# One core, top-k attention and mixer MLP: the closing check in five blocks at other places, planner figures for transfers, and a new order of steps

## The chip, the cores and the metric

The kernel runs on one core of a Trainium2 chip. The core has TensorE (PE, with its weight loads shown as PEld), VectorE (DVE), ScalarE (ACT), GpSimd (POOL) and SyncE (SP, which here only issues transfers). Each engine takes its own instructions in program order and waits for others by semaphores. The metric is device time in microseconds (us), from launch to end; smaller is better.

## The reference

Eight batches of eight heads, 576 rows of 64 numbers each. For every row the 32 largest scores are kept, the softmax runs over these, and the result goes through two MLPs, one across the 576 tokens and one across the 512 channels.

```python
scores = scale * np.matmul(q, k.transpose(0, 1, 3, 2))
kth = np.partition(scores, -top_k, axis=-1)[..., -top_k:-top_k + 1]
scores = np.where(scores >= kth, scores, -1000000000.0)
attn = np.exp(scores - np.max(scores, axis=-1, keepdims=True))
attn = attn / (np.sum(attn, axis=-1, keepdims=True) + 1e-09)
x = heads side by side of np.matmul(attn, v)          # 8 x 576 x 512
h = np.maximum(x.transpose(0, 2, 1) @ w_tok1, 0.0) @ w_tok2
u = x + h.transpose(0, 2, 1)
out = u + np.maximum(u @ w_ch1, 0.0) @ w_ch2
```

## The kernel before

**Tiling.** Two heads of a batch make a pair, so there are 32 pairs; a pair has nine tiles of 128 rows by 576 scores, 288 tiles in all, and two tiles are worked on together as a duo. Two pairs share one duo, since 576 is four and a half times 128. `group` takes one or two duos, `front` loads and transposes q and k of a pair, `back` multiplies by v, and `mlp_ops` runs the MLPs of a batch after every fourth pair.

**One duo.** TensorE makes the scores (L553), ScalarE copies them on a grid of whole numbers into the tile SX (L368). VectorE finds the largest values in six segments (L590, L593, L594, L596) and from them a first threshold, with small steps on a handful of numbers (L686, nh). ScalarE counts how many scores lie above it (L608, into `cnt`). GpSimd turns the scores into integers around that threshold (L616, L619), VectorE finds the eight largest of these (L625, into `tlo`), and small steps give the final threshold (L686 nt, L707). Then there are two ways on. Most duos are rescored: GpSimd marks the kept scores in U (L634), TensorE forms the scores once more with the dropped ones pushed down (L563, L569), and ScalarE takes the exponential into Pm (L639). The others (KEEP) have their exponential from before (L601), and GpSimd makes a mask M and multiplies (L645, L649). SP transposes Pm by a transfer into PT (L671). Only the last duo (number 286 of the rows' count) is transposed by TensorE, in `flip` (L662), with a copy by ScalarE (L666) and one by VectorE (L668). `back` multiplies PT by v (L730) into a bank of TensorE's memory, and VectorE divides by the row sums (L744 reciprocal, L747 product, into Xb). The bank is free again after L747.

**The MLPs.** L794 and L809 are the first token product, L829 and L833 the second with the residual, L916 and L949 the first channel product, L868 and L873 the second with the residual; L799, L838, L886, L936, L944 and L962 are ScalarE's copies and ramps behind them, and L881, L889, L954 and L957 VectorE's share in the last batch. The last batch begins part of L916 ahead of time in held chunks.

**The check.** The threshold search holds for data within bounds. At the end the kernel checks the bounds on `cnt`, `thi`, `tlo` and the row sums `rds` and adds the violations in `bad`; TensorE sums them over the 128 rows (L1038), VectorE casts the sum to `flag` (L1041). If the flag is above 0, the whole is computed again by a slow path (L1184 on, not run with these inputs). `judge` (L1007 to L1028) is one step of 21 VectorE instructions, with 6.0 us in the plan; `sums` (L1030) follows after the last division. `tmp` and `ti`, which `judge` writes, lie in the two buffers of sg, the unused output of L608. The inputs of `judge` are complete once the last L625 is done.

**The order.** Each piece of work is a step: `plan.add` gets the engine, a duration, the function that issues the instructions, the steps that it depends on and the buffers that it uses. `ORDER` holds two characters for every step, which give its place. `Plan.run` goes through the steps by place, adds up a time for each engine and each buffer from the durations, picks for every buffer the one that comes free first by this reckoning, and puts warm-up products (`heat`, L1046) into TensorE's gaps. It does not reorder. The dependencies given to `plan.add` enter this reckoning only; the waits in the program are set where instructions touch the same data. `CLOG` is a charge on SP's steps while earlier transfers still run; `dma` of `weight` says how long a transfer of weights occupies the transfer engines in the plan. The weights are issued by GpSimd (`wdma`, L410).

**VectorE's order at the end, before.** The last L625; the last group's L686 and L707; `judge`; L744 and L747 of the pair 30; the copy L668; L744 and L747 of pair 31, in three parts; `sums`; four L954 and four L957; L889; L881; L881; the flag; L881. GpSimd's order at the end: U of duos 282, 280 and the first half of 286; M; a cast of v (L465); M; the second half of U of 286; two L649. TensorE's: L730 of pair 30; the rescores of 280 and 286; L794; L868 in two halves; `flip`; L829; L730 of pair 31 in two parts (40 and 10 products), with held chunks of L916 between; L794; the rest of the MLPs.

Of the kernel before, what the change touches and what calls it, by code (L numbers as in the profile page):

```python
# [19 lines left out]
LOWEST = -(2.0**33) + 2.0**12  # L20
HIGHEST = 2.0**34 - 2.0**12
# [20 lines left out]
    "'$'''c'd'o's(}'l'm(O(r(~$g$o$x%L$}$~%H%0%Y&/&?%$%|%M%/%<&,&:&>&E$h$q%F%G%{%}&)%]&+&0&H%6&%%z&-&'%D&=&M&O&R'5'8':"
    "'9'F'D'L'e'j'h'x(%'k'g'f(-(4(9(C(E(w(y)#(D(F)$)I*&***5*8#3#4#1$/$0$=$>#a&U&W(|'3'2'7'6,?%N%P%W&<&1&w&#&K&~'%'*&5"
    "&8&G&@&I&r'-'0'E%O%Q&C&J&x&o&v&{'&'/'H%_&2&F&N&B&6')'J'O%x'R't'q'r'p('(Z(((,(@(A(=(P(](?(G(B(`(f(h(n)5)G)H)L)Z*("
    ")P)S)Q)V*)%q%t&7&z&D&t&q'#','I'U&P'S&Q'M&}'+'['`'w&j&l&|'V'Q'G'P'W'Z'b'~&n'.'(&p'C&s'K'|($()(J(M(I(L(R(^(i)D)C)E"
    ")b)e)F)R)N)g)m)x*+*-*.*a*c*,*U*b*d*y'?'A'N'a'Y(0(3(1(6(:(<'T']'{'z(#'y(&(*(Q(u(Y({(v)-)<)@)U)O)T)}*;*=*A*H*W*Y*X"
    "*Z*z+J+W+['@'B'^(5(;'_(X(S(a(c),'X'}(+(/(o(p)&)+)4'n'u(8(d(V(U(W(k(m)*)7(7(l(j(g(_(b).)3):)=)X)`)W)[*6*$*4*S*R*Q"
    "*h*m*V+%*T*u+.+4+K+N,$,(,-+O+R,),,,.(H(K(T)8)0)6([)%)?)h)l(e)>);)9)/)f)k)q)s(x(z)))c)n)r)i)1)u)w)|)')2)d)p)o)()t"
    ")z*#*0*[*]*^*_*p*o*v+'+M+&+D+U+(+Q+L+]+`+c,*,+,/,2-#,:,;,O,Q,~-;-G-K(N(q*P*`,%,&-g-j(s(t*g+$,0,3-l.N-m.O.R.U.S.X"
    "/V/Z.n/E/T/^.h/_/U/Y0h1B0i1C0k1@1{1~1|2#2^2m2t333c3{5t5B5|6j5c5f627$$(&X-r)A)B)J)K/?'<*'&S*f*e*~*}-[)M)Y)v)y*M*<"  # L50
    '*3*I*k*n*w)j*1*7*/){*@*B*s+/)])_)~*i*r*C*:*D*t+7+;*9*J*G*E+2*F+6+9+A+#+C+I+H+G+F+_,K+d+l,9,7,8,A,F,<,=,6,L,N,T,p'
    ',q,r,s-(-7-n,z-X,|-Y-s)^)a*2*N*>*?*j*q+=+h+m*K*x*O+5*L*l+:+e+o+)+++0+1+?+3+^+<+f+k+q+8+>+V+Y+X+T+b+p+s+u,4,1,5,R'
    ",a,g,k,v,x,y-0-3,{,},w-=-D-S-]-_.Q.T/8-`-b.Y.f/9+*+,+B+z+j+y+Z+g,G,J,_+@,C+}+w+x,E,I,M,e,',l-9-6-B-M-Q-Z-a-^.A.C"
    '.E.G.I.`.d.c.e/:/a/l/n+-+E+i+v+~+|,D+{,H,`,i+a,B+n+t,#+r,W,f,m,@,P,S,Z,Y,c,V,X,j,n-),U,[,d,^,],b,h,o-?-A-c-d-i-k'
    ".;.3.:.[.].^.o.r._.b.a.z/./2/C/D/b/|00/}/~0/020b-$-'-+---O-.-R-2-U.#.%-*-L-1-,-/-4-V.&.1-:-<-E-I-P-z-|-x.,.5.8-H"
    '-{-}-J-W-T.-.7.<.@.V.k.W.i/(.{/+/</@/=/K/Q/B/>/A/c/e/z0(0)050X0c0,0-0]0^0d1`1e1h*%*|-q,t,u-&-%1E-o-t2a.g.m.j.}4+'
    "-5-8->.*.2.(.0-N.?.t.w-@.)-F.'-~-C.4.6.y-e-f-w.D.9./.K.$.p.s.~-v.=.+.B.M-y.q/#/%.P/)/X/[/F/G/j/g/f/k0&0'0%0:0E0*"
    "0+0$0H0L0P0S0p1I1M1r1t2`1G1J1H1a2_-h-u.>/&.F.H.L.v/-/R/t...u.J/$.x/P/u/w07.l.|/'///*/7/6/4/J/O09/,/1/I/3/0/5/h08"
    "0?0A0[0W0e0Y1.1,141K1N1L1S1[1Q1O1P1j1l1n1x1y2X2]2c1z2Y2d2r3'/;/H/S0@0B/p/i/o0G0R0T/L/N0F/M/d/q0n0q0|/`1+1=1>1R1U"
    "1Z1b1d1c1o2%2,22252Z2e2[2f2n393S3V/W/]/m/s0>/x0C/v0N0U1#/r0V0I0o0O/y0z1*1//{0.0;0Q0l0x0M0=0{1'150<0J0m0u0w0D1$1-"  # L60
    '191<2$1v1A1D2G2B2F2h2i2g2z2}2k2l2j3$3<3@3^3_3z3~443]3`3}4-4503040r121)100t0v181:1]0K131X1%160~1_1m2-060Z0s1&110y'
    '1V0}1q2.211(1W1;1T1^171g1p24292q2p2o2s3#2|3&3-3/3.3B3D3132303F3H3J3a3b4,40464)4*4N4X4l5e6)686f6l6h6n7(7I717Z7X7['
    "7Y7]9#9,9/9490969d9o8~939c9l:D:X9e9n:C:W9g9p:E:Y:~;D;A<(;@;Y;T<*;]<);S;[<'<-<3<4<@<{=@=u@F=5=B=w=A=C=y?8-p*{3(0`"
    "0_0f0g4P0a2b5q3+3*3534700j1?1i2:2)2+2C282L2Q2U1Y1k1f2*2'2E2H2T2W1s1u2&2I2;2(202D2P2S2w2<2V2>2@2=2?2x2{2~363%373Y"
    "3e3Z3j4B3i3p4%4&4$4:4=4'4(4#4?4A4J4L4M4Q4R4s4t5o4S4U4T4V5p1w1}232M272N2K2J2R3C3T2/2v2y2O2A263=3N3m2u3,3?3K3M3I3O"
    '3G3Q3W3r3;3L3>3E3X3A3l3q3t3v484u4/4r595=5@5F5H5G5Q5T5J5K5I5X5[5`5k5l656g6i5j5m6m6~7#383:3P4H3k3U3R3y4[4c4g3h4@3u'
# [102 lines left out]

# [1066 lines left out]
```

## Time and profile before

| | us |
|---|---|
| median of three runs | 744.05 |
| lowest and highest of them | 742.95, 744.85 |
| the profiled execution | 743.19 |
| its span, first to last instruction | 741.2 |

The page gives busy time by engine over the span. A stretch is a part of the span between two times. The order in time lists an engine's instructions as start, duration, engine, line, operation, output and inputs, and in brackets how long the engine was idle before it and what ended that. The chain that ended last is followed back from the last instruction, at each step to what released it. An instruction's busy time holds any stall inside it.

### The profile page before, as it was taken

What the parts mean: (1) busy time and instruction counts of PE and PEld (TensorE: products, weight loads), DVE (VectorE), ACT (ScalarE), POOL (GpSimd) and SP (SyncE); (2) the same over time, 40 slices, a digit from 0 to 9 for tenths busy, and PEclk for the clock granted to TensorE, in tenths of its full rate; (3) what the DMA queues carried; (4) which work ended last, traced back from release to release, by engine and by line L of the source; (5) the groups of instructions that cost most, each with busy time, mean ns of one, the idle gap of its engine ahead of it and who ended that gap; (6) DMA issues with size and microseconds to landing.
All of it is one profiled execution on the core that took longest, in us unless ns stands there. A gap on an engine that the chain in (4) does not pass through costs nothing.

```text
span 741.2 us, 22242 instructions
## 1 busy us (share of the span) xinstructions
PE 685.5 (92%) x7434; PEld 381.7 (51%) x7502; DVE 672.4 (91%) x3812; ACT 659.6 (89%) x1134; POOL 635.8 (86%) x867
## 2 busy tenths in 40 slices
...
GB/s 133 112 135 123 132 143 181 95 127 139 165 130 152 90 108 143 179 121 84 111 142 103 84 160 117 137 123 164 110 105 106 178 108 134 94 97 123 88 44 62
DMA packets 286715, 90.45 MB, mean 122 GB/s; under 512 B 273024, under 2 KB 283136, under 8 KB 286592
## 3 DMA queue, kind: packets, MB, share of 16 engines
...
q8 instruction: 61, 1.00, 0.6%
...
q10 hardware_dynamic: 800, 0.20, 0.1%
...
## 4 chain that ended last, share of the span: by engine, by line
DVE 37%; PE 26%; ACT 17%; POOL 10%; issue 4%; DMA 4%; SPq 0%; ACTq 0%; POOLq 0%; DVEq 0%
DVE cd L590 16%; DVE tlo L625 11%; PE bank L916 6%; ACT sg L608 5%; ACT SX L368 5%; PE bank L868 5%; POOL SX L616 4%; PE bank L553 4%; ACT Pm L639 4%; PE bank L569 4%; DVE cd L594 2%; POOL Pm L649 2%; POOL U L634 2%; DMA PT<-Pm 2%; DMA kL<-in_k_dram 2%
## 5 line engine op out<-in xcount | busy, mean ns | idle before, releaser
L590 DVE MAX8 cd<-SX 128x8 f32<-128x96 f32 x1728 | 342.1, 245 | 7.0 <-ACT SX L368 6.6
L616 POOL TENSOR_SCALAR SX<-SX,nh,gs 128x576 int32<-128x576 f32 x288 | 234.2, 820 | 10.7 <-DVE gs L686 5.8
L625 DVE MAX8 tlo<-SX 128x8 uint32<-128x584 uint32 x288 | 218.8, 760 | 13.8 <-POOL SX L616 6.7
L608 ACT ACTIVATE sg<-SX,nh 128x576 bf16<-128x576 f32 x288 | 224.6, 787 | 1.8 <-DVE nh L686 1.1
L553 PE MATMUL bank<-kT,qT 64*64 64x288 f32 x2304 | 173.9, 416 | 10.7 <-ACT SX L368 4.3
L634 POOL TENSOR_SCALAR U<-SX,nt,ws 128x576 uint8<-128x576 int32 x200 | 162.5, 823 | 19.1 <-DVE nt L686 10.9
L368 ACT ACTIVATE SX<-bank 128x1152 f32<-128x1152 f32 (+1 forms) x147 | 162.8, 1117 | 11.7 <-PE bank L553 10.6
L639 ACT ACTIVATE Pm<-bank 128x1152 bf16<-128x1152 f32 x100 | 113.4, 1135 | 21.4 <-PE bank L569 16.5
L569 PE MATMUL bank<-kT,qT 64*128 64x288 f32 x800 | 126.2, 434 | 0.0
L553 PEld LDWEIGHTS bank<-kT,qT 64*64 64x64 f32 x2304 | 76.5, 132 | 87.1 <-ACT SX L368 15.9
L649 POOL TENSOR_TENSOR Pm<-E,M 128x576 bf16<-128x576 bf16 x88 | 111.2, 1277 | 6.4 <-ACT SX L368 4.6
L916 PE MATMUL bank<-UT,wc1b 128*128 128x512 bf16 x355 | 87.9, 379 | 3.2 <-ACT SX L368 1.0
L868 PE MATMUL bank<-wc2b,H 128*128 128x512 bf16 x360 | 88.6, 383 | 2.3 <-issue 1.3
L569 PEld LDWEIGHTS bank<-kT,qT 64*128 64x128 f32 x800 | 69.8, 188 | 32.7 <-issue 22.4
L645 POOL TENSOR_SCALAR M<-SX,no,ws 128x576 int8<-128x576 int32 x88 | 72.0, 823 | 2.5 <-DVE no L707 1.9
L608 ACT ACTIVATION_READ_ACCUMULATOR sg<-SX,nh 128x1 f32 x288 | 60.3, 209 | 0.0
L868 PEld LDWEIGHTS <-H 128*128 128x128 bf16 x384 | 35.0, 99 | 48.0 <-issue 14.2
L916 PEld LDWEIGHTS <-wc1b 128*128 128x128 bf16 x380 | 34.9, 98 | 46.5 <-issue 11.4
L730 PEld LDWEIGHTS <-PT 128*128 128x128 bf16 x1600 | 52.3, 98 | 12.4 <-issue 7.7
L730 PE MATMUL bank<-vb,PT 128*128 128x65 bf16 x1600 | 55.2, 194 | 3.3 <-ACT Pm L639 1.2
L563 PE MATMUL bank<-U,identN 64*64 64x288 bf16 x800 | 44.6, 295 | 14.2 <-DVE Xb L747 5.0
L601 ACT ACTIVATE E<-SX,lift 128x1152 bf16<-128x1152 f32 x44 | 55.9, 1270 | 0.0
...
## 6 DMA issues: line engine op xcount, KB each, us to landing
...
```

The source lines that it names most:

```text
L368: nc.scalar.activation(out=dst, in_=src, func=AF.Copy, scale=GRID, bias=-LEVEL * GRID)
L553: nc.tensor.matmul(out=row(s1.t, h, lo, lo + HS, c, 64), lhsT=x["qT"].t[r, q0 : q0 + 64], rhs=x["kT"].t[r, lo : lo + HS], start=True, stop ...
L569: nc.tensor.matmul(out=row(s2.t, h, lo, lo + HS), lhsT=x["qT"].t[r, q0 : q0 + P], rhs=x["kT"].t[r, lo : lo + HS], start=False, stop=True)
L590: ss.append(plan.add("DVE", 0.06 + (bounds[a + 1] - bounds[a]) / 960, lambda a=a, h=h, cd=cd: nc.vector.max(cd.t[:, a, :], Sb.t[:, h, boun ...
L608: got.append(plan.add("ACT", 0.761, lambda i=i0 + 1 - h, h=h, sg=sg: nc.scalar.activation(out=sg.t[:, :], in_=Sb.t[:, h, 0:S], func=AF.Sig ...
L616: xo.append(plan.add("POOL", 0.805, lambda i=i0 + 1 - h, h=h: nc.gpsimd.tensor_scalar(out=xi(Sb)[:, h, 0:S], in0=Sb.t[:, h, 0:S], scalar1= ...
L625: mxs.append(plan.add("DVE", 0.674, lambda i=i0 + 1 - h, h=h: nc.vector.max(tlo[:, at(i) - 7 : at(i) + 1], Sb.t[:, h, :].bitcast(u32)), [d ...
L634: us.append(plan.add("POOL", 0.805, lambda i=i0 + 1 - h, h=h: nc.gpsimd.tensor_scalar(out=byte(U.t[:, h, :], 1), in0=xi(Sb)[:, h, 0:S], sc ...
L639: oe = [plan.add("ACT", 1.013, lambda: nc.scalar.activation(out=Pm.t[:, :, 0:S], in_=pairs(s2.t), func=AF.Exp, scale=scale), [orr], use=[s ...
L649: oe.append(plan.add("POOL", 1.262, lambda h=h, M=M: nc.gpsimd.tensor_tensor(out=Pm.t[:, h, 0:S], in0=E.t[:, h, :], in1=M.t[:, :], op=ALU. ...
L868: nc.tensor.matmul(out=po, lhsT=H.t[:, fc, r0 : r0 + P], rhs=wc2b[:, fc, :], start=(fc == 0), stop=(rows is not None and fc == NF - 1))
L916: nc.tensor.matmul(out=o, lhsT=wc1b[:, cc, fc * P : (fc + 1) * P], rhs=UT.t[:, cc, :], start=(cc == 0), stop=(cc == (hi if whole else NC) ...
```

## The change

`judge` is split into five steps, `depths`, `parity`, `window`, `lowest` and `floors`, with the same 21 instructions; the order among them changes in that the two bounds on `thi` come first. The plan's durations are 1.4, 1.35, 1.4, 0.95 and 1.25. In the plan `depths` depends on the maxima `tops` alone; the other four depend on `lasts`, on each other in this order, and on the GpSimd step that was added last (`spent`, the second half of U of duo 286). In the plan the weights' transfers occupy 4.0 us instead of 2.6 and `CLOG` is 0.6 instead of 0.25. `ORDER` is a new list with four more entries.

```diff
-    FAR, CLOG = 0.06, 0.25
+    FAR, CLOG = 0.06, 0.6
...
-    def weight(key, at, lat, f, acq=(), dma=2.6):
+    def weight(key, at, lat, f, acq=(), dma=4.0):
...
-    def judge():
+    def depths():
         nc.vector.memset(ones[:, :], 1.0)
+        nc.vector.tensor_reduce(out=bad[:, 4:5], in_=thi[:, 7 : NT + 7], op=ALU.max, axis=AX.X)
+        nc.vector.tensor_scalar(out=bad[:, 4:5], in0=bad[:, 4:5], scalar1=HIGHEST, scalar2=None, op0=ALU.is_gt)
+        nc.vector.tensor_reduce(out=bad[:, 5:6], in_=thi[:, 7 : NT + 7], op=ALU.min, axis=AX.X)
+        nc.vector.tensor_scalar(out=bad[:, 5:6], in0=bad[:, 5:6], scalar1=LOWEST, scalar2=None, op0=ALU.is_lt)
+
+    def parity():
         nc.vector.tensor_scalar(out=ti, in0=cnt[:, :], scalar1=0.5, scalar2=None, op0=ALU.mult)
...
+    def window():
         nc.vector.tensor_scalar(out=tmp, in0=cnt[:, :], scalar1=513.0, scalar2=None, op0=ALU.add)
...
+    def lowest():
         nc.vector.tensor_copy(out=tmp, in_=tli[:, 7 : NT + 7])
...
+    def floors():
         nc.vector.scalar_tensor_tensor(out=tmp, in0=tmp, scalar=2.0, in1=thi[:, 7 : NT + 7],
                                        op0=ALU.mult, op1=ALU.add)
...
-    jd = plan.add("DVE", 6.0, judge, lasts)
+    jd = plan.add("DVE", 1.4, depths, tops)
+    spent = [o for o in plan.ops if o.eng == "POOL"][-1:]
+    for step, dur in ((parity, 1.35), (window, 1.4), (lowest, 0.95), (floors, 1.25)):
+        jd = plan.add("DVE", dur, step, lasts + spent + [jd])
     jd = plan.add("DVE", 0.6, sums, [jd] + mixed[B - 1])
```

Read as places, the new list differs from the old one in the position of most VectorE steps (3221 of 3479 that both have), by 8 positions on average; of TensorE's 593 steps 149 stand elsewhere. At the end VectorE's order becomes: `depths` between two L625 of duo 280; the last L625; the last group's L686 and L707; L744 and L747 of pair 30; L668; `parity`; L744 and L747 of pair 31; `window`; `lowest`; four L954, three L957, `floors`, the last L957; L889; `sums`; three L881; the flag. GpSimd's ends with both halves of U of 286, then M, L649, M, L649; the cast of v stands earlier. On TensorE `flip` moves between the two halves of L868, and one held chunk of L916 moves behind the last L794. On ScalarE the copy L666 of the flipped tile moves behind a copy L886 and a copy L838.

More of the change, by code (lines that the diff above doesn't have):

```diff
@@ L42 @@
[L42 to L66, printed above, removed]
@@ new lines @@
+    "#e#k#o#x#v#m#p$'$7$;#i#}#t#r#n#u$&$3$L#d#f#q$$#y$#$%#s$4$:$Z#w#|#{#~$5#z$8$I$a$c$y$x$v$w%1%5%8%h%k%g%|%~%i%p%m&$"
+    "&'&)&Y&[&h&j':&X&Z'-'0'8$/$1$J$k$j$P$b$K%)%-%0$N%#$T%($g%%%3%6%<%I%B%G%H%_%^%f%q%r%o&+&/&:&?&Q&a&e&c&f'9'u(+(1$G"
+    '$R$V%.$[$f%*$d%2%;%@$W%&$}$|$i$Y%4%:%X$H$S$_%N%L$`$e%R%U%Y%[${%P%K$~%+%/%W%]%a%d%v%z%x%{&9&6&F&^&`&_&p&w&]&d&b&z'
+    "')'E'b'c'n't(u'd'k(O(k(w$l$u%,%=%S%7%>%M%e&-&1%$%'&0%9%V&,&4&B&E$m$z%?&2&7%J%A&&&=&A&K%O%}&#%T%c%Z&%&D&P&S'?'4'="
+    "'2'G'D'R'e'h'f'~(%'i'g'j(2(:(=(C(D(o(q(y(F(G(z)M*,*2*=*?#2#4#1$.$0$=$>#b&W$)*-'/'.'3'1,>%D%F%`%b&N&>&O&@&n&s&|&("
@@ new lines @@
+    "&H&*&t&C&v&~'$'(%C%E&3&y&<&x&R&5'%'''*%Q&M&l&T&G&8&r&{'C%y'N'q'o'p's(')9(,(3(@(B(A(P(W(?(>(E(_(c(e)/);)G)L)P)^*/"
+    ")S)V)T)W*.%s%w&I&L'&&q&}&J','F'V&.'Q&;'K'P'O'Y'^'x&g&i&k'W'B'J&m'H'Z'y'{&o'I'S'+'#&u'U']'}(((M(I(J(L([(T(g)E)J)I"
+    ")d)f)H)F)K)j)o)r*4*5*:*g*j*3*7*i*k*|';'>'L'M(#'z($(8(;(Q(S'A'X(*'|'w(&(4(9(b(n(i(s(t)A)1)5)U)X)R)t)v*&*B*G*]*`*_"
+    "*a*}+P+W+X'<'@'T(|(`'[(X(^(~)%).'_(/(Y'v(.(6(h)()4'm'r()(a(5({(7)&),)2)7(-(0(<(Z(V(d)#)-):)?)[)Z)Y)_){*%***6*8*9"
+    "*M*p*b+&*^*z+3+9+Q+R,#,&,,+U+V,(,+,-(H(K(U)*(}(f)$)))0)6)i(R)e)8)+)'(])m)x)|(p(r)=)@)B)g)h)k)n)u)~)3)s)q)l)>)<)w"
@@ new lines @@
+    ")}*$*(*e*c*h*d*u*r*x+(+,+)+G+J+'+T+++Z+_+a,),*,.,1,z,5,9,L,O,{-:-L-O(N(j*[*f,$,%-l-n(l(m*n+%,/,2-p.Q-o.R.T.W.U.Y"
+    "/Y/].p/G/W/a.r/`/X/[0p1@0m1B0o1C1y1|1x1{2a2p2v323^3{4i5F5w6g5d5x65<4'5(v-v)C)D)O)N.g(x'7'6*m*l+$+#._)Q)]*#*@*'*)"
+    '*N*R*X*o*{)p*I)z*S)y*>*W*w+:)`)b*E*J*F*s*P*t*y+7+>*D*U*O*K*Q*V*Z*q+A+0+H+O+N+M+L+j+v+k+n,6,:,7,@,G,;,<,8,J,P,S,c'
+    ',k,o,p-%-6-s,x-]-[-^-t)a)c*+*L*;*<*A*C*v+6+I*H*T+<+C*Y+B+Y+c+i+-+/+;+]+?+@+=+[+e+h+l+4+f+E+b+8+5+g+m+p+u,4,0,3,N'
+    ",^,V,_,q,w,r-'-.,u,y,v-0-3-?-a-c.S.V/:-d-e.[.j/;+.+1+D+`+w+x+z+F+},K,Q+o,B+y+r+|,A,D,H,],',d-7-#-A-H-M-_-b-`.'.+"
@@ new lines @@
+    '.6.:.?.c.h.e.i/</c/m/p+2+K+d,R+t,F+q,I,Y,[,g+^+s+{+~,E,C,W,Z-&,?,M,U,a,f,X,`,e,i,m-+,T,h,j,b,n,l-*---4-=-f-h-g-m'
+    '.#.0.A.a.].b.s.w.d.^.f.{/1/5/E/F/d/~020#0$00040f,|-$-(-<-2-1-)-B-N-V-{-,-S-I-/->-F-Z-~.%-9-;-C-x-E-Q-}-T.&.(.1-@'
+    "-X-Y.$-P-|.,./.4.7.X.l.Z.m/*.~/'/?/A/>/L/N/C/@/B/Q/h/u0)0*070_0g0-0.0b0c0h1[1d1f*0*~/9,s,t,~,}1a-q-u03.k.q.n/$3["
+    "-5-8-D-U.2-R.5-K.>.C.J-G.<-J-W.-.B.F.H.L-i-j...@.O.9.K.N.u.y.|-y.D.3.E.=-z.v.z/%.P/)/H/^/J/I/j/x/f/o0&0%0'0;0B0("
+    '0,0+0G0I0N0R0W1J1K1n1p2d1F1H1G1I2b-k-w.).x.}.G.I.t///O/T.*/&.8.;.M/3/g/i/{.o/#/(/M/8/./4/0/P/y09/+/7/,/6/-/2/t/z'
```

175 lines of the change are left out of this document (88 added, 87 removed).

## The prediction, made before the changed kernel was run

> **What bounds the kernel now.** I read the page's totals, then busy time by stretches, then the order in time on each engine around the closing check, then the chain that ended last.
>
> ```profile
> span 741.2 us, 22242 instructions
> PE 685.5 (92%) x7434; PEld 381.7 (51%) x7502; DVE 672.4 (91%) x3812; ACT 659.6 (89%) x1134; POOL 635.8 (86%) x867
> ```
> ```profile
> 150.00:665.00 515.00, 493.65 (x5522) 276.75 (x5575) 498.77 (x2867) 498.48 (x860) 482.54 (x651) 1.00 0.67 126
> 665.00:687.40 22.40, 21.95 (x196) 12.10 (x196) 15.64 (x27) 12.75 (x24) 20.74 (x27) 1.00 0.54 125
> ```
>
> A stretch's columns are its length, the busy time of PE, PEld, DVE, ACT and POOL, and the granted clock. From 150 to 665 us no engine stands out: VectorE has 16.2 us free, TensorE 21.4. From 665 to 687.4 us TensorE is full (21.95 of 22.40) and VectorE is not. Then comes a hole. These are the orders in time of DVE, of POOL and of PE around it:
>
> ```profile
> 679.23 6.68 DVE L1009 TENSOR_SCALAR sg<-cnt 128x288 int32<-128x288 f32 x1
> ...
> 685.94 0.46 DVE L1010 SCALAR_TENSOR_TENSOR sg<-sg,cnt 128x288 f32<-128x288 int32 x1
> ...
> 686.92 0.31 DVE L1013 TENSOR_SCALAR sg<-cnt 128x288 f32<-128x288 f32 x1
> ...
> 690.25 0.44 DVE L1024 TENSOR_REDUCE bad<-thi 128x1 f32<-128x288 f32 x1
> ...
> 691.55 0.22 DVE L744 RECIPROCAL rds<-bank 128x10 f32<-128x10 f32 x1
> 691.80 0.82 DVE L747 TENSOR_TENSOR Xb<-bank,rds 128x640 bf16<-128x640 f32 x1
> ```
> ```profile
> 676.95 3.23 POOL L634 TENSOR_SCALAR U<-SX,nt,ws 128x576 uint8<-128x576 int32 x4
> ...
> 683.24 2.51 POOL L649 TENSOR_TENSOR Pm<-E,M 128x576 bf16<-128x576 bf16 x2
> ```
> ```profile
> 684.18 1.69 PE L730 MATMUL bank<-vb,PT 128*128 128x65 bf16 x50
> 685.80 0.44 PE L563 MATMUL bank<-U,identN 64*64 64x288 bf16 x8
> 686.17 1.24 PE L569 MATMUL bank<-kT,qT 64*128 64x288 f32 x8
> 687.34 0.31 PE L563 MATMUL bank<-U,identN 64*64 64x288 bf16 x1
> 692.68 0.69 PE L563 MATMUL bank<-U,identN 64*64 64x288 bf16 x7 [5.03 <-DVE Xb L747]
> ```
>
> L1009, the check's first operation on 288 numbers, takes 6.68 us. L1013, of the same kind and length with a float result, takes 0.31. L1009 ends at 685.91 and GpSimd's last operation at 685.75. So it stood still while GpSimd worked, through a row of operations, not through one. The check is one block, 679.23 to about 691.5, and behind it on VectorE stands the division of the last pair but one (L744, L747). Its sums were ready at 685.87 (end of L730); it starts at 691.55. TensorE, which needs the bank that L747 frees, waits **5.03 us**. The hole has a second price, in the chain of work and in the stretch behind it:
>
> ```profile
> 692.68 0.69 PE bank L563 x7
> 693.37 2.22 PE bank L569 x8
> 695.59 1.18 PE bank L794 x10
> 696.77 0.22 issue
> 696.99 3.46 PE bank L868 x11
> ...
> 700.68 0.56 PE bank L662 x10
> ...
> 701.89 1.22 PE bank L730 x40
> ...
> 707.31 0.56 PE bank L794 x10
> ...
> 716.24 2.37 PE bank L868 x11
> ```
> ```profile
> 692.70:700.70 8.00, 7.78 (x44) 4.29 (x45) 0.00 (x0) 1.41 (x2) 0.00 (x0) 0.62 0.01 2
> ```
>
> The granted clock is 0.62 there, against 1.00 ahead of the hole. The same groups at full clock: seven of L563 0.32 (eight take 685.80 to 686.17), eight of L569 1.17 (to 687.34), ten of L794 0.56, eleven of L868 2.37. The excess is 0.37 + 1.05 + 0.62 + 1.09 = **3.13 us**, and 0.22 of issue time.
>
> [...]
>
> **The change part by part.** *The split check.* Read off the new list, VectorE's steps at the end run: depths between two of the last L625; the last group's L686 and L707; then at once L744 and L747 of the last pair but one; the copy L668; parity; the last pair's divisions; window; lowest; L954 and L957, with floors ahead of the last L957; L889; sums; three L881; the flag. Ahead of the division that TensorE waits for, of the whole check only depths is left. Nothing is removed: all operations still run. The wait for GpSimd is an entry in the planner's list of dependencies, by which the list was fitted; in the program a wait comes from data, and none of the four blocks reads what GpSimd wrote last. Their place does it: parity stands behind L668, which copies what the last rescore led to, and that rescore needs the last U, behind which GpSimd has two M and two Pm left (0.81 and 1.26 each by the rows above, 4.1). From that U to L668's end lie a rescore 1.54, an exp 1.13, a flip 0.56 and the copy 0.49, 3.7 with no wait counted, and TensorE comes to that rescore only 4 us after the U. So parity meets an idle GpSimd.
>
> The division can start at 685.87 and some 0.2, and ends by 687.2. TensorE stands at 687.34, so the hole closes. It goes on at full clock: the rescore to 688.9, L794 to 689.4, six of L868's twelve (1.3) to 690.7, the flip L662, which the list now puts between the halves, to 691.3, the other half with its identities (1.5) to 692.8, L829 and L833 (701.89 - 700.68 - 0.56 = 0.65) to 693.45. Then L730 x40, which began at 701.89. Two other inputs have to be there. The flip needs the last exp: 688.9, and 0.16 as between L569's end and L639 below, and 1.13 is 690.2, against 690.7. L730 x40 needs a transpose of what the exp below leaves at 688.63; it lands 3.4 later, at 692.0, 1.4 ahead of its use.
>
> ```profile
> 687.50 1.13 ACT L639 ACTIVATE Pm<-bank 128x1152 bf16<-128x1152 f32 x1 [2.05 <-issue]
> ```
> ```profile
> DMA to landing us min/median/max: 3.4/3.4/4.2
> ```
>
> On ScalarE the copy L666 now stands behind L886 and L838; it is done near 695.0, and the ten L730 that need it come near 696.7. Behind L730 TensorE's steps are the same, in nearly the same order (one held chunk passes the last L794), so the rest of the program comes forward by as much: 5.03 + 3.13 + 0.22 = **8.38 us**.
>
> *Where the blocks lie now.* By starts, parity is 685.94 to 686.92 and 0.35 for L1009 without its stall, 1.33; window, lowest and floors together 686.92 to 690.25, 3.33, of which floors is about 1.2 by the planner's shares; depths at most 690.25 to 691.55, 1.3.
>
> ```profile
> 703.22 0.20 DVE L744 RECIPROCAL rds<-bank 128x6 f32<-128x6 f32 x1 [1.40 <-PE bank L730]
> ...
> 710.71 1.92 DVE L954 TENSOR_TENSOR H<-bank,SX 128x512 bf16<-128x512 f32 x3 [4.22 <-PE bank L851]
> ...
> 713.34 0.68 DVE L957 TENSOR_SCALAR H<-H 128x512 bf16<-128x512 bf16 x3
> ...
> 728.87 0.69 DVE L881 TENSOR_TENSOR ob<-bank,SX 128x512 f32<-128x512 f32 x1 [2.07 <-PE bank L868]
> ```
>
> Parity fits the 1.40 that VectorE waits ahead of L744; window and lowest (2.1) fit the 4.22 ahead of L954. Floors puts the last L957 from 714.02 to 715.2, and L868, which reads it, started at 716.24. Sums (0.6 in the plan) fits an idle stretch like the 2.07 ahead of an L881. The flag's copy, now behind the last L881, falls near 729.6, and the last store is issued at 733.64. All are taken at nothing; TensorE's own work hides them, and without that cover they cost 1.3, 2.1, 1.2 and 0.6.
>
> ```profile
> 733.64 1.18 SPq L970 DMA_DIRECT2D out_dram<-ob  x2
> ```
>
> *Depths* is taken at nothing too, since VectorE has room after 665 us. But its two comparisons of one number each have not been seen beside a busy GpSimd. Bounds: L686, 6 or 12 numbers, never over 0.17 in the whole run; and L1009's 6.68. I take the first, the row of nearly the same length.
>
> ```profile
> L686 DVE TENSOR_SCALAR nt<-tlo x80: 135/148/167, 23.0 to 678.7; 128x12 f32<-128x12 int32 x64, 128x6 f32<-128x6 int32 x16
> ```
>
> *Longer transfers and the larger CLOG* are figures of the planner; no transfer changes. The last chunk of wc1b is issued at 95.9 and first used at 120.3: nothing waits for it, nothing is won.
>
> ```profile
> L410 POOL DMA_DIRECT2D wc1b<-in_moe_w_ch_dram x4: 553/576/612, 53.5 to 95.9; - x4
> ```
> ```profile
> L916 PE MATMUL bank<-UT,wc1b x355: 376/379/390, 120.3 to 715.0; 128*128 128x512 bf16 x178
> ```
>
> *The list fitted anew.* Most VectorE steps change place by a few positions, few of TensorE's do. The work is the same, and no row prices an order. At best it wins VectorE's 16.2 us of air; on the other side each wait of GpSimd's U for a late nt has cost up to 3.6. I take nothing, as the engines' work is unchanged and they are full, and 3 us either way for the range.
>
> ```profile
> POOL U L634 <- DVE nt L686: 10.9, 10, 3.6
> ```
>
> **The sum.** The profiled execution took 743.19 (span 741.2 and 1.99 around it), which gives 734.8. It lies 0.86 under the median of the runs; 744.05 - 8.38 = **735.7**.
>
> **The rivals.** *The clock stays low.* The hole closes, but TensorE meets another wait in the same stretch (the margin of 1.4 us is thin) and runs slow again: 744.05 - 5.03 = 739.0. For it: 0.62 is what a long wait brought here. Against: every input I could place is in time.
>
> *Depths stalls.* GpSimd has no pause there (20.74 busy from 665 to its end at 685.75), so a comparison held like L1009 holds VectorE until GpSimd runs dry, at the U whose nt stands behind depths. Then three L625 pass (0.76 each) and as much again of small steps and refilling, about 4 us as an estimate, of which 1.4 is cover: 735.7 + 2.6 = 738.3. Against: L686.
>
> ```profile
> L625 DVE MAX8 tlo<-SX 128x8 uint32<-128x584 uint32 x288 | 218.8, 760 | 13.8 <-POOL SX L616 6.7
> ```
>
> *The slowness is L1009's own* and moves into parity with it: 6.3 us more between L668 (done about 692.0) and L744 (wanted at 693.45 + 1.22 + 0.2 = 694.9). Done at 692.0 + 1.3 + 6.3 = 699.6, it makes TensorE 4.7 late: 740.4, and with 3.1 of slow clock again 743.5. Against: its end lies 0.16 behind GpSimd's. [...]
>
> *Slower: the new list loses in the body.* Place: 150 to 665 us, where TensorE has 4% free. Price: 3.6 for each late nt that leaves GpSimd empty long enough to reach TensorE. It takes three of these, 10.8, to eat 8.38 and to pass the 2.2 that can be measured: 746.5 and more. For it: most VectorE steps moved, and the planner's buffers are dealt out anew. Against: ten such waits cost 10.9 together before, and were mostly hidden.
>
> *The list wins 3 us or more:* 732.7 and less, since 16.2 us of air are there to be had.
>
> **How the numbers follow.** Forecast 0.57, low clock 0.12, depths 0.09, L1009 itself 0.04, body loses 0.06, list wins 3 or more 0.12. Forecast, low clock and depths, each with the list's 3 us, ask for 732.7 to 741; the range is 732.0 to 741.0, and what it leaves out is the body's loss, half of L1009's and half of the list's win, under 0.2. A measurement of this kernel can tell 0.3%, 2.2 us, so faster is under 741.8: 0.88, with the low clock and depths on that side for the most part; same 0.06; slower 0.06.
>
> **What would show it.** Right: L1009 near 0.35, after GpSimd's last operation; no wait of L563 for L747; a clock near 1.00 through the last rescore, L794 and L868; L730 x40 some 8.4 us earlier against the span. For depths, L1025 and L1027 near 0.15. Wrong: L1009 again near 6; parity, window or floors named as the releaser of a TensorE wait; or the last rescore itself reached more than 3 us away from 687.34, which is the list's doing and not the check's.

## The result, and the profile after

The changed kernel takes 731.49 us (median of four runs, 730.85 to 731.98). The kernel before took 744.45 on the same chip (four runs, 742.95 to 744.87). The ratio is 0.9829, with an interval of 0.9812 to 0.9846; by it, 12.7 us are gone. The forecast had 8.4 of them, and 731.49 lies just below its range, 732.0 to 741.0. The profiled execution of the changed kernel took 730.85, its span 729.0.

First the place that the forecast was about. These are the changed kernel's first lines of the page, then its busy time by stretches (columns as before: length, busy time of PE, PEld, DVE, ACT and POOL, granted clock, share of the DMA engines, GB/s).

```profile
span 729.0 us, 22359 instructions
PE 686.2 (94%) x7516; PEld 380.3 (52%) x7516; DVE 665.6 (91%) x3812; ACT 659.5 (90%) x1134; POOL 635.9 (87%) x867
```
```profile
150.00:665.00 515.00, 500.57 (x5590) 278.07 (x5589) 500.95 (x2878) 501.87 (x870) 485.51 (x657) 1.00 0.65 126
...
680.00:692.00 12.00, 12.00 (x173) 8.05 (x171) 3.79 (x10) 4.88 (x7) 1.55 (x2) 1.00 0.63 121
692.00:716.00 24.00, 24.00 (x182) 13.05 (x181) 9.45 (x26) 9.43 (x19) 0.00 (x0) 1.00 0.24 56
```

The order in time of VectorE, then of TensorE, around the division of the last pair but one:

```profile
681.69 0.22 DVE L744 RECIPROCAL rds<-bank 128x10 f32<-128x10 f32 x1 [6.20 <-PE bank L730]
681.94 0.82 DVE L747 TENSOR_TENSOR Xb<-bank,rds 128x640 bf16<-128x640 f32 x1
...
688.03 0.30 DVE L1015 TENSOR_SCALAR sg<-cnt 128x288 int32<-128x288 f32 x1
688.37 0.46 DVE L1016 SCALAR_TENSOR_TENSOR sg<-sg,cnt 128x288 f32<-128x288 int32 x1
```
```profile
681.51 0.44 PE L563 MATMUL bank<-U,identN 64*64 64x288 bf16 x8
681.88 1.24 PE L569 MATMUL bank<-kT,qT 64*128 64x288 f32 x8
683.05 0.44 PE L563 MATMUL bank<-U,identN 64*64 64x288 bf16 x8
683.42 1.24 PE L569 MATMUL bank<-kT,qT 64*128 64x288 f32 x8
```

L1015 is the check's first operation on 288 numbers, L1009 of before: 0.30 us and not 6.68. The division waits for nothing but its sums, no wait stands ahead of the last rescore's L563, TensorE is busy through all of 680 to 716 us, and the clock is 1.00. From the end of the last L625 to the end of the span, before has 741.2 - 678.65 = 62.55 us and after 729.0 - 674.90 = 54.10. **The tail gave 8.45 us; 8.38 were forecast.**

The rest is ahead of the tail: the last L625 itself ends 3.75 us earlier. Counting the 288 L625 as milestones shows where (k counts from 0; the end of each, in us; an ordinary listing of the trace's rows, not a view):

```
k      before    after   difference
45     123.41   120.81     -2.60
54     140.25   140.17     -0.08
63     162.65   158.84     -3.81
72     183.69   180.15     -3.54
287    678.65   674.90     -3.75
```

Differences come and go until k = 54; what appears between 54 and 63 stays, give or take an order that differs, to the end. So there is one hole in the kernel before, and the forecast did not see it. The 8.45 of the tail and these 3.75 add up to the 12.2 between the two profiled spans. These are the kernel before's busy time in 150 to 160 us, its waits in 140 to 160 (engine, line, waited for: us, times, longest) and GpSimd's order in time:

```profile
150.00:160.00 10.00, 7.96 (x110) 4.37 (x112) 6.80 (x37) 7.12 (x14) 6.92 (x10) 1.00 0.60 104
```
```profile
POOL Pm L649 <- ACT SX L368: 4.6, 1, 4.6
DVE tlo L625 <- POOL SX L619: 3.2, 1, 3.2
```
```profile
145.15 0.81 POOL L410 DMA_DIRECT2D wc2b<-in_moe_w_ch_dram  x1
146.01 1.62 POOL L645 TENSOR_SCALAR M<-SX,no,ws 128x576 int8<-128x576 int32 x2
147.62 0.81 POOL L634 TENSOR_SCALAR U<-SX,nt,ws 128x576 uint8<-128x576 int32 x1
153.08 1.28 POOL L649 TENSOR_TENSOR Pm<-E,M 128x576 bf16<-128x576 bf16 x1 [4.64 <-ACT SX L368]
```

The same two views of the changed kernel, and what SyncE issues there:

```profile
150.00:160.00 10.00, 9.08 (x115) 5.03 (x113) 10.00 (x57) 9.52 (x20) 9.92 (x16) 1.00 0.82 165
```
```profile
143.97 0.79 POOL L410 DMA_DIRECT2D wc2b<-in_moe_w_ch_dram  x1
145.16 1.62 POOL L645 TENSOR_SCALAR M<-SX,no,ws 128x576 int8<-128x576 int32 x2 [0.41 <-DVE no L707]
147.05 2.51 POOL L649 TENSOR_TENSOR Pm<-E,M 128x576 bf16<-128x576 bf16 x2 [0.26 <-DMA PT<-Pm]
```
```profile
143.24 9.12 SPq L671 DMA_TRANSPOSE PT<-Pm  x4
```

VectorE is busy 6.80 of the ten microseconds before and 10.00 after. L649 writes Pm, the buffer that a transposing transfer (L671) reads; in both kernels it starts only behind that transfer's landing, by 0.17 us before and 0.25 after. The page puts its wait down to ScalarE's L368, which had long been done; the landing times name the transfer instead. Each row is one transfer, from its issue to its landing:

```
                  issued   landed   us
before  L410      145.15   151.81   6.7   last chunk of wc2b
        L671      145.51   152.91   7.4   transposing transfer of Pm
after   L671      143.24   146.80   3.6   transposing transfer of Pm
        L410      143.97   150.79   6.8   last chunk of wc2b
        L671      144.75   151.89   7.1   the next transposing transfer
```

Before, the chunk goes out 0.36 us ahead of the transfer, which then takes 7.4 us. After, the transfer goes out first and takes 3.6. The collision has not gone: the next transposing transfer, issued 0.78 us behind the chunk, takes 7.1 there. But VectorE loses nothing by it there: it is busy for the full ten microseconds.

### The profile page after: what moved, and what is told of

It reads as the page before. It is cut to its first block, busy times and chain, and to the rows that moved or that the text cites. A ratio compares the mean times of both kernels' runs of the same rounds, so it can differ in the third digit from the quotient of the medians.

```text
span 729.0 us, 22359 instructions
## 1 busy us (share of the span) xinstructions
PE 686.2 (94%) x7516; PEld 380.3 (52%) x7516; DVE 665.6 (91%) x3812; ACT 659.5 (90%) x1134; POOL 635.9 (87%) x867
## 4 chain that ended last, share of the span: by engine, by line
DVE 56%; PE 19%; ACT 14%; POOL 6%; issue 3%; DMA 1%; SPq 0%; ACTq 0%; POOLq 0%; DVEq 0%
DVE cd L590 25%; DVE tlo L625 17%; PE bank L868 5%; PE bank L916 5%; ACT sg L608 4%; DVE cd L594 4%; ACT SX L368 3%; POOL SX L616 3%; DVE thi L596 3%; PE bank L569 2%; ACT Pm L639 2%; DVE m L593 2%; DVE Xb L747 2%; ACT H L962 2%; PE bank L553 2%
## 5 line engine op out<-in xcount | busy, mean ns | idle before, releaser
L625 DVE MAX8 tlo<-SX 128x8 uint32<-128x584 uint32 x288 | 218.7, 759 | 9.7 <-POOL SX L619 4.5
L553 PE MATMUL bank<-kT,qT 64*64 64x288 f32 x2304 | 172.1, 414 | 13.6 <-ACT SX L368 7.5
L368 ACT ACTIVATE SX<-bank 128x1152 f32<-128x1152 f32 (+1 forms) x147 | 162.6, 1117 | 9.7 <-PE bank L553 7.8
L569 PE MATMUL bank<-kT,qT 64*128 64x288 f32 x800 | 124.1, 429 | 0.0
L649 POOL TENSOR_TENSOR Pm<-E,M 128x576 bf16<-128x576 bf16 x88 | 111.3, 1278 | 3.0 <-ACT kT L534 1.3
L868 PE MATMUL bank<-wc2b,H 128*128 128x512 bf16 x384 | 91.3, 380 | 0.1
L916 PE MATMUL bank<-UT,wc1b 128*128 128x512 bf16 x380 | 90.1, 379 | 1.3 <-ACT SX L368 1.2
L868 PEld LDWEIGHTS <-H 128*128 128x128 bf16 x384 | 34.6, 98 | 46.8 <-issue 13.0
L916 PEld LDWEIGHTS <-wc1b 128*128 128x128 bf16 x380 | 34.6, 98 | 46.5 <-issue 11.9
L596 DVE MAX8 thi<-cd 128x8 f32<-128x36 f32 x288 | 53.8, 187 | 1.0
```

What stands on the lines that cost most here:

```text
L368: nc.scalar.activation(out=dst, in_=src, func=AF.Copy, scale=GRID, bias=-LEVEL * GRID)
L553: nc.tensor.matmul(out=row(s1.t, h, lo, lo + HS, c, 64), lhsT=x["qT"].t[r, q0 : q0 + 64], rhs=x["kT"].t[r, lo : lo + HS], start=True, stop ...
L569: nc.tensor.matmul(out=row(s2.t, h, lo, lo + HS), lhsT=x["qT"].t[r, q0 : q0 + P], rhs=x["kT"].t[r, lo : lo + HS], start=False, stop=True)
L625: mxs.append(plan.add("DVE", 0.674, lambda i=i0 + 1 - h, h=h: nc.vector.max(tlo[:, at(i) - 7 : at(i) + 1], Sb.t[:, h, :].bitcast(u32)), [d ...
L649: oe.append(plan.add("POOL", 1.262, lambda h=h, M=M: nc.gpsimd.tensor_tensor(out=Pm.t[:, h, 0:S], in0=E.t[:, h, :], in1=M.t[:, :], op=ALU. ...
L868: nc.tensor.matmul(out=po, lhsT=H.t[:, fc, r0 : r0 + P], rhs=wc2b[:, fc, :], start=(fc == 0), stop=(rows is not None and fc == NF - 1))
```

## The experiments

Two theories came out of this. One: the last chunk's place ahead of a transposing transfer made the hole near 150 us. The other: with the check ahead of L744, its first operation on 288 counts (`sg<-cnt`, which the expectations call the first two-port operation; that is a name, no run here shows ports) stands still until GpSimd runs dry, and splitting the check is what cures the tail. The first was borne out, the second only by half. The letters that name theories in the expectations hold for the group of runs that they stand in.

### The check cut in five, old list (e1), and the chunk alone (e2)

e1 keeps the old list and puts the five blocks where the changed kernel has them.

```diff
+    behind(step(parity), dve[j + 3])
+    w = step(window)
+    behind(w, dve[j + 9])
+    behind(step(lowest), w)
+    behind(step(floors), dve[j + 17])
+    behind(jd1, dve[j + 19])
```

> The kernel before, old list and old planner figures; only the check is cut into the five blocks and parity, window, lowest, floors and sums are issued behind L668, the last division, L957 and L889 as in the changed kernel (depths stays where judge was). Theory A (the check's stall cost 5.03 us of waiting and 3.13 us of slow clock, and the other gain came from elsewhere): 736.1 us, 8.4 below 744.45, no wait of L563 for L747, clock 1.00 behind 687 us, the body unchanged (last L625 ending near 678.7). Rival B (the whole gain of 13 us is the check's, the list does not matter): 731.5. Rival C (the clock stays slow): about 739.

Measured: 737.00 us, ratio 0.9894 [0.9859, 0.9928], 7.9 us gained. TensorE has no wait for L747, and the first operation takes 0.30. From the last L625 to the end of the span are 734.2 - 679.93 = 54.27 us, 8.28 less than before.

e2 keeps the check whole and issues the last chunk of wc2b four of GpSimd's steps later.

```diff
+    pool = [o for o in order if isinstance(o, Op) and o.eng == "POOL"]
+    c = wl["c2"][-1]
+    behind(c, pool[pool.index(c) + 4])
```

> The kernel before, with one instruction moved: the last weight chunk (the fourth transfer of wc2b, issued at 145.15 us) is issued four GpSimd steps later, behind the L649 that waited 4.64 us for its buffer. Theory A (that chunk, issued just ahead of the transposes L671, held them and by them Pm, GpSimd and VectorE): the wait of L649 shrinks below 1 us, the transpose issued near 145.5 lands after some 4 us instead of 7.4, VectorE has no hole between 150 and 160, and the program takes 740.9, 3.5 below 744.45. Rival B (the loads of k and q queued on SP ahead of these transposes did it, not the weights): the wait stays near 4, 744.4. Rival C (the hole is won but given back to a later wait): hole gone, 743 to 744.

Measured: 742.63 us, ratio 0.9965 [0.9944, 0.9986], 2.6 us gained where 3.5 were expected. In the profiled execution, which at 739.98 is one of its fastest, the last L625 comes 2.2 us earlier. Busy time in 150 to 160 us, GpSimd's order, and the check's first operation:

```profile
150.00:160.00 10.00, 9.75 (x128) 5.18 (x127) 9.75 (x53) 9.58 (x20) 9.95 (x14) 1.00 0.63 107
```
```profile
149.93 1.28 POOL L649 TENSOR_TENSOR Pm<-E,M 128x576 bf16<-128x576 bf16 x1 [0.88 <-DMA PT<-Pm]
151.15 0.81 POOL L410 DMA_DIRECT2D wc2b<-in_moe_w_ch_dram  x1
```
```profile
677.02 6.71 DVE L1009 TENSOR_SCALAR sg<-cnt 128x288 int32<-128x288 f32 x1
```

With the chunk behind L649, the transfer takes 3.9 us (issued 145.87, landed 149.76), L649 waits 0.88 and VectorE has 9.75 of the ten. The hole is closed by one transfer's place. The tail's hole is there as before.

### Both (e3), and the changed kernel with the check in one piece (e4)

e3 holds both edits.

> The kernel before with both edits, the blocks of e1 and the chunk of e2, still on the old list and figures. If the two gains are independent and are all there is: 744.45 - 8.4 - 3.5 = 732.5, within 1.5 of the changed kernel's 731.49. If the new order in the rest has a gain of its own: 2 us or more above the changed kernel.

Measured: 735.04 us, ratio 0.987 [0.9835, 0.9904], 9.7 us gained; tail 54.28 us, last L625 at 677.92, which is 2.0 earlier than in e1, where only the chunk differs. The changed kernel has its last L625 3.0 us earlier still, so the new list may hold something beyond the last chunk. Of these 3.0, 1.3 are there at k = 54 (141.50 against 140.17, where the kernel before has 140.25), 0.6 come between 54 and 63, and 1.1 behind: no second hole.

e4 is the other way round: the new list, but the check whole again and ahead of L744.

```diff
+    for o in parts[1:4] + parts[:1] + parts[4:]:
+        behind(o, mark)
+        mark = o
```

> The changed kernel with the five blocks issued in one piece again, in judge's order, ahead of the division L744 of the last pair but one; list and planner figures new. Theory A: the first operation stalls until GpSimd's last one, TensorE waits some 5 us for L747 and runs slow behind it: 731.49 + 8.4 = 739.9. Rival (with the new list the place no longer matters, since GpSimd finishes earlier): under 734.

Measured: 733.61 us, ratio 0.9848 [0.9814, 0.9882]. Putting the check back costs 2.1 us by the medians (1.4 by the ratios, whose intervals overlap), and not 8.4. From the last L625 to the end are 730.3 - 674.80 = 55.5 us, so 7.1 of the tail's 8.45 are won without the split. The order on VectorE and TensorE:

```profile
675.30 0.47 DVE L1015 TENSOR_SCALAR sg<-cnt 128x288 int32<-128x288 f32 x1
675.81 0.96 DVE L1016 SCALAR_TENSOR_TENSOR sg<-sg,cnt 128x288 f32<-128x288 int32 x1
677.29 0.34 DVE L1021 TENSOR_SCALAR sg<-cnt 128x288 f32<-128x288 f32 x1
677.66 0.96 DVE L1022 TENSOR_TENSOR sg<-sg 128x288 f32<-128x288 f32 x1
```
```profile
684.21 0.43 PE L563 MATMUL bank<-U,identN 64*64 64x288 bf16 x7 [1.01 <-DVE Xb L747]
```

GpSimd works until 681.98 here, and the check's operations get through all the same. The two with two inputs in these lines (L1016, L1022) take 0.96 instead of 0.46, and each ends 0.30 us behind the end of the GpSimd operation that was running when it started: each waits for one operation of GpSimd, not for all. TensorE waits 1.01 us and the clock stays at 1.00. **So the second theory falls as it stood**: the split is one cure, the new list another. They do not add up: by the ratios, of 744.45 us, the split alone is worth 7.9 (e1), the list alone 11.3 (e4), both 12.7.

### What makes the first operation stand still?

Nine runs change one thing each; they look for what lets the operation through on the new list and not on the old. In each pair of diffs, the first is made to the kernel before and the second to e4.

*The memset.* In the old order the memset of `ones` stands right ahead of the operation. (e5 takes it away from there; e6, with no diff here, puts it there in e4.)

```diff
 def judge():
-        nc.vector.memset(ones[:, :], 1.0)
...
+        nc.vector.memset(ones[:, :], 1.0)
```

> The kernel before, in which only the memset of `ones`, the instruction right ahead of the check's first operation, stands behind the check's last operation instead. Nothing else is moved. Theory M (the check's first operation was passed over by seven operations of GpSimd because of what stands right ahead of it, the memset): it takes under 1 us as in the changed kernel with the check in one piece (0.47 us), the other operations of the check wait for at most one operation of GpSimd each, TensorE's wait for L747 goes from 5.5 us to about 1 us, no clock is lost, and the time is about 737.5 us (744.5 less some 7). Theory P (how the two engines' operations happen to stand to each other decides, or something else in the old order): the operation takes 6.7 us again and the time is 744.5 +- 1.5 us.

> The changed kernel with the check in one piece ahead of L744 (as in e4_back, 733.6 us), and the memset of `ones` right ahead of its first operation, as the kernel before has it. Theory M: the first operation now takes about 6 us, to the end of GpSimd's last operation, TensorE waits some 5 us for L747 and loses clock behind it, and the time is 738 to 741 us. Theory P: 0.5 us as in e4_back and 733.6 +- 1 us.

Measured: e5 745.37 us, ratio 1.0 [0.9981, 1.0019], and 6.72 us for the operation; e6 733.50, 0.9856 [0.9821, 0.9891], and 0.47. **It is not the memset.**

*The moment of the start.*

```diff
 def judge():
+        nc.vector.tensor_reduce(out=bad[:, 4:5], in_=thi[:, 7 : NT + 7], op=ALU.max, axis=AX.X)
...
         nc.vector.tensor_scalar(out=ti, in0=cnt[:, :], scalar1=0.5, scalar2=None, op0=ALU.mult)
```
```diff
 def parity():
+        nc.vector.tensor_scalar(out=bad[:, 6:7], in0=cnt[:, 0:1], scalar1=0.5, scalar2=None, op0=ALU.mult)
+        nc.vector.tensor_scalar(out=bad[:, 7:8], in0=cnt[:, 0:1], scalar1=0.5, scalar2=None, op0=ALU.mult)
```

> The kernel before, in which the check's two TENSOR_REDUCE over thi (with the two small operations behind them) stand at its head and not near its end; the check is still one piece ahead of L744. Its first two-port operation (sg<-cnt) then starts about 1 us later, in the middle of an operation of GpSimd and not 0.15 to 0.17 us ahead of one's end, as it did in all four runs of the old order that were passed over (0.15, 0.16, 0.17, 0.16), against 0.30 and 0.31 in the two runs where it went through in 0.47 us. Theory S (the moment of the start against the end of GpSimd's running operation decides): it takes at most 1 us, the check ends some 5 us earlier, TensorE's wait for L747 is 1 us or less, 737 to 738 us. Theory O (something else in the old order makes it wait until GpSimd has nothing left): it takes 5 to 6 us, to GpSimd's end, and the time is 743.5 to 744.5 us.

> The changed kernel with its check in one piece ahead of L744 (as e4_back, 733.6 us), and two operations on one column put ahead of the first two-port one, which moves its start by about 0.14 us, from 0.30 to some 0.16 us ahead of the end of GpSimd's running operation. They compute nothing that is used. Theory S: it is passed over until GpSimd's last operation (about 6 us), and the time is 738 to 741 us. Theory O: 0.3 to 0.5 us, and 733.6 +- 1 us.

Measured: e9 743.66 us, ratio 0.9987 [0.9967, 1.0008]; e10 733.08, 0.9849 [0.9818, 0.9881]. VectorE's order in e9, then in e10:

```profile
680.21 5.59 DVE L1013 TENSOR_SCALAR sg<-cnt 128x288 int32<-128x288 f32 x1
685.84 0.46 DVE L1014 SCALAR_TENSOR_TENSOR sg<-sg,cnt 128x288 f32<-128x288 int32 x1
```
```profile
676.51 0.35 DVE L1017 TENSOR_SCALAR sg<-cnt 128x288 int32<-128x288 f32 x1
676.90 0.95 DVE L1018 SCALAR_TENSOR_TENSOR sg<-sg,cnt 128x288 f32<-128x288 int32 x1
```

Started a microsecond later, it stands still until GpSimd's end all the same; moved to 0.19 us ahead of the end of a GpSimd operation, near the old moment (0.15 to 0.17), it goes through. Two runs further down close the gap between these: it starts 0.22 us ahead of such an end in e15 and stands still, and 0.23 ahead in e16 and goes through. **It is not the moment** against GpSimd's running operation.

*GpSimd's last operations.* (e14, with no diff here, has e9's four operations twice and one of them once more.)

```diff
+    r = pool[-11:]
+    behind(r[6], r[0])
+    behind(r[8], r[4])
+    behind(r[5], r[9])
```
```diff
+    r = pool[-12:]
+    behind(r[0], r[8])
+    behind(r[10], r[0])
+    behind(r[7], r[10])
```

> The kernel before, in which only GpSimd's last nine operations are put into the order that the changed kernel gives them (the five L634 first, then L645, L649, L645, L649, with L465 ahead of them); the check is untouched, one piece ahead of L744. Theory R (the order of GpSimd's last operations decides: in the old one most of them post nothing at their end, in the new one each posts a semaphore): the check's first two-port operation takes under 1 us, the check ends 4 to 5 us earlier and the time is 737 to 739 us. Theory V (it is something of VectorE's own order or of the rest of the old list): 6 us again and 744.5 +- 1 us.

> The changed kernel with its check in one piece ahead of L744 (e4_back, 733.6 us) and GpSimd's last operations in the order of the kernel before (L634, L645, L465, L645, L634, L649, L649). Theory R: the first two-port operation is passed over to GpSimd's end, TensorE waits 4 to 5 us for L747, and the time is 738 to 741 us. Theory V: under 1 us, and 733.6 +- 1 us.

> The kernel before, in which the check begins with its four operations over thi done twice and one of them once more, so that the first two-port operation starts about 2.7 us later, inside GpSimd's second L645, the first operation of the old row that posts a semaphore at its end. Theory U (an operation of GpSimd that posts at its end lets the waiting VectorE in there, one that posts nothing does not): it takes under 1 us. If not: it takes 3.5 to 4 us, to GpSimd's end. The time by itself says little, 743 to 745 us, since 1.6 us of work are added.

Measured: e12 742.53 us, ratio 0.9963 [0.9947, 0.9978]; e13 731.54, 0.9824 [0.9799, 0.9849]; e14 744.05 in its one run. The first operation in e12, in e13, and in e14:

```profile
680.86 2.06 DVE L1009 TENSOR_SCALAR sg<-cnt 128x288 int32<-128x288 f32 x1
```
```profile
675.33 0.47 DVE L1015 TENSOR_SCALAR sg<-cnt 128x288 int32<-128x288 f32 x1
```
```profile
684.64 4.02 DVE L1018 TENSOR_SCALAR sg<-cnt 128x288 int32<-128x288 f32 x1
```

The new row shortens the stall to 2.06 us in the old list, which neither theory had forecast, so the row has a part in it; the old row does not bring it into the new list. In e14 two operations of GpSimd that post a semaphore end while it waits (at 685.23 and 686.03) and do not let it in: posting is not it either.

*VectorE's own steps ahead of the check.*

```diff
+    behind(dve[j - 2], dve[j - 5])
```
```diff
+    behind(dve[j - 4], dve[j - 2])
```

> The kernel before, in which one small operation of VectorE (L686, ws<-cnt) stands two places earlier, so that VectorE comes to the check by ws, nt, no, no, as in the changed kernel, and not by nt, no, ws, no. Theory V (what VectorE does right ahead of the check decides): the first two-port operation takes under 1 us and this one run about 737 to 739 us. Otherwise 5 to 7 us, to GpSimd's end, and 744.5 +- 2 us; then the cause is outside VectorE's own order.

> The changed kernel with its check in one piece ahead of L744 (e4_back, 733.6 us), with VectorE's operations ahead of it in the order of the kernel before (nt, no, ws, no). Theory V: the first two-port operation is passed over to GpSimd's end, 738 to 741 us. Otherwise under 1 us and 733 +- 1.5 us.

Measured, one run each: e15 744.69 us and 6.76 for the operation; e16 733.83 and 0.39. **It is not VectorE's order.**

So: with the whole check ahead of L744, eight runs on the old list (before, e2, e5, e8, e9, e12, e14, e15) show the stall, in seven of them to 0.17 us behind GpSimd's last operation; five on the new list (e4, e6, e10, e13, e16) do not, with 0.35 to 0.47. What in the list decides it **stays open**. A rival that was not tried is the data's buffers, which the planner deals out along with the list. By the kernels' own planner, GpSimd's last operations use the same SX buffers (0, 1, 2 and 5) in all eight runs that stall, and others (1, 2, 4 and 8) in all five that do not; so they go with the outcome in every run, as the list does.

### The chunk the other way (e7), and the planner's figures alone (e8)

e7 is the changed kernel with its last chunk of wc2b ahead of the transposing transfer, as e2 turned round.

```diff
+    behind(c, pool[pool.index(c) - 4])
```

> The changed kernel, in which only the issue of the last chunk of wc2b stands four operations of GpSimd earlier, so that it is issued ahead of the transposing transfer of Pm and not behind it. Theory A (a weight chunk that is under way when a transposing transfer of Pm is issued holds that transfer, Pm's buffer, L649 and with it VectorE): L649 waits 3 to 4 us near 147 us, the transfer takes about 7 us instead of 3.6, and the time is 734 to 735 us. Theory B (the hole of the kernel before came from the rest of its order, and the chunk's place does not matter): no such wait, 731.5 +- 1 us.

Measured: 734.21 us, ratio 0.9865 [0.9836, 0.9895], 2.7 us slower than the changed kernel by the medians. GpSimd's order, and busy time in 150 to 160 us:

```profile
148.94 2.52 POOL L649 TENSOR_TENSOR Pm<-E,M 128x576 bf16<-128x576 bf16 x2 [2.08 <-DMA PT<-Pm]
```
```profile
150.00:160.00 10.00, 8.24 (x109) 4.75 (x108) 8.33 (x44) 8.24 (x17) 10.00 (x16) 1.00 0.87 125
```

The chunk goes out at 141.44, the transfer at 142.91 and lands at 148.69, 5.8 us later; L649 waits 2.08, less than the 3 to 4 expected, and VectorE loses 1.67 of the ten. The L625 with k = 63 is 1.94 us later than in the changed kernel, the last one 1.87: a delay made here is never caught up. **Moving the chunk alone closes the hole in the one kernel and opens one in the other.**

> The kernel before with only the planner's two figures changed (CLOG 0.6 for 0.25, a transfer of a weight chunk counted as 4.0 us for 2.6), and its old list of orders. The issue order of the named operations stays as the list has it, so the figures alone can act only through the warm-up products and the choice of buffers. Theory A: the last chunk of wc2b keeps its place, the hole near 150 us stays, and the time is 744.5 +- 0.7 us. Rival: the figures move chunks by themselves and fill the hole, 741 us or less.

```diff
-    FAR, CLOG = 0.06, 0.25
+    FAR, CLOG = 0.06, 0.6
...
-    def weight(key, at, lat, f, acq=(), dma=2.6):
+    def weight(key, at, lat, f, acq=(), dma=4.0):
```

Measured: 745.85 us, ratio 1.0022 [1.0004, 1.0039]. L649 still waits 3.56 us there, until 155.55. The figures by themselves win nothing; if they do something, it is by the list that was fitted under them.

### A faster version? (e11, e17)

Two pairs of warm-up products (L1057) lie on the changed kernel's chain that ended last:

```profile
713.60 0.75 PE bank L1057 x3
714.36 2.59 PE bank L868 x12
716.95 0.43 PE bank L1057 x2
```

e11 leaves out those behind the check.

```diff
+        late = late or f is jd
+        if isinstance(f, Op):
+            f.fn()
+        elif not late:
+            f()
```

> The changed kernel without the five warm-up products (L1057) behind the check's last step; nothing else is changed. They stand on the chain of waits with 0.75 and 0.43 us. If they delay the products behind them, 1.18 us go: 730.3 us. If the products behind them wait for ScalarE's H at those places anyway, nothing goes: 731.5 us. If the clock falls without them, up to 1 us is lost: 732.5 us.

> The changed kernel with both edits that looked a little faster by themselves: GpSimd's last operations in the order of the kernel before (e13 had 731.5 us with the check in one piece, 2 us below e4) and no warm-up products behind the check (e11, 731.0 us). If the order's 2 us are won in the changed kernel as well: 729 us. If the split check has won them already: 731 us, as e11.

Measured: e11 730.99 us, ratio 0.9806 [0.9789, 0.9823]; e17 731.90, 0.9823 [0.9796, 0.9851]. In e11 the 24 products then stand together on that chain:

```profile
715.04 0.12 PE bank L1049 x2
715.16 5.29 PE bank L868 x24
```

From L1049 to the last L868 are 5.40 us, against 6.49 in the changed kernel (713.48 to 719.97); the whole tail is 0.7 shorter. But the last L625 of e11 came 1.55 us later than in the changed kernel, and the trace shows where: the hole near 150 us came back in part, with the list unchanged. These are GpSimd's L649 and the busy time there:

```profile
148.88 2.52 POOL L649 TENSOR_TENSOR Pm<-E,M 128x576 bf16<-128x576 bf16 x2 [2.16 <-ACT kT L534]
```
```profile
150.00:160.00 10.00, 8.46 (x109) 4.81 (x108) 8.29 (x44) 8.33 (x17) 10.00 (x16) 1.00 0.99 161
```

The transposing transfer was issued at 143.24, 0.67 us ahead of the chunk, and still landed only at 148.63, 5.4 us later; in the changed kernel it was 0.73 ahead and took 3.6. So going out first does not always save the transfer, and the new list leaves it little margin. e17, with the same products left out, is no faster than the changed kernel. A gain of under 1 us is possible for e11 and not established; no run beats the changed kernel clearly.

## Why the prediction was right and wrong

**The tail was right in size.** 5.03 + 3.13 + 0.22 = 8.38 stood against 8.45 in the changed kernel and 8.28 in e1, where only the check was cut. Parity's first operation took 0.30 ("near 0.35"), no wait of L563 for L747 was left, the clock was 1.00, and *depths* at nothing held: its comparisons beside a busy GpSimd took 0.15. "The clock stays low" and "depths stalls" are out. That 8.45 came so near is no proof of the reason given, since under the new list two cures act on the same hole.

**The step that failed** is the list's term: "I take nothing, as the engines' work is unchanged and they are full". For the planner's figures alone, "nothing waits for it, nothing is won" held (e8). But the list fitted under them moved the last chunk of wc2b from ahead of a transposing transfer to behind it. The prediction asked who waits for a chunk's data, and found no one. It did not ask whom a chunk's transfer holds up while it is under way. In the kernel before that was a transposing transfer, by it Pm's buffer, by it GpSimd, by it VectorE. It also looked at the last chunk of wc1b and not at wc2b's. The bound was there to be read: 6.80 of VectorE's ten microseconds from 150 us, hidden in a mean over 515 us. The list's term, taken as 0 with 3 either way, measured 3.75 us: the last chunk about 2 of it (2.2 by e2 against before, 2.0 by e3 against e1, in one profiled execution each). The rest could not be traced to one place; runs on the old list with the chunk untouched differ among themselves in the end of the last L625 by some 2.8 us (678.53 in e9, 681.36 in e5), so a microsecond or two of it may be such variation. The list also has a part in the tail, as e4 showed. The rival "the list wins 3 us or more: 732.7 and less", at 0.12, is what happened. Its own sign came true: the last rescore starts at 683.05, more than 3 us away from 687.34, "the list's doing and not the check's".

**The reason for the tail was wrong in part.** "Their place does it", the prediction says of the blocks. It does in e1. But e4 has the check in its old place and only 2.1 us come back, and none in e13 (731.54), so under the new list the place is not needed to free the tail. That L1009 stood still "through a row of operations, not through one" describes the old list's runs (6.68 us and seven operations of GpSimd). In e4 the operations that waited did so for one operation of GpSimd (0.96 against 0.46); no run shows what decides between the two. "The slowness is L1009's own" is out: the same operation takes 0.35 in e10 beside a busy GpSimd.

**The clock's price** was right for that wait, but the mean of 0.62 over 8 us hides its form. These are the stretches behind the wait in the kernel before, then in e12 (a wait of 2.36 us), then in e4 (1.01 us), with the mean granted clock ahead of the last two columns:

```profile
692.10:698.80 6.70, 5.90 (x30) 3.27 (x31) 0.52 (x1) 1.41 (x2) 0.00 (x0) 0.50 0.01 2
698.90:704.90 6.00, 5.95 (x77) 3.89 (x76) 1.61 (x5) 1.76 (x3) 0.00 (x0) 1.00 0.22 89
```
```profile
692.10:695.40 3.30, 3.30 (x19) 2.22 (x20) 0.00 (x0) 0.00 (x0) 0.00 (x0) 0.50 0.32 59
695.50:700.00 4.50, 4.50 (x54) 2.94 (x53) 0.49 (x1) 2.98 (x5) 0.00 (x0) 1.00 0.07 25
```
```profile
684.20:692.20 8.00, 7.99 (x100) 5.30 (x100) 0.88 (x3) 3.17 (x5) 0.00 (x0) 1.00 0.59 103
```

In these stretches the clock reads 0.50 or 1.00. It was at 0.50 for 6.8 us in the kernel before (692.1 to 698.9) and for 3.4 us in e12; e4 lost the wait alone. The wait's length does not settle it: in the 8 us behind the wait the mean clock was 0.81 after 3.95 us in e9, 0.71 after 4.04 in e14 and 0.78 after 5.14 in e5.
